# Three edits made together: the order of x's scalings and of h's sums at four seams, the stores of the derived output weights, and the last product of the output; with them, one tile in another bank and one order of products

## The chip, the cores and the metric

One core of a Trainium2 chip runs the whole program. The metric is the device time of one execution in microseconds (us), the median over several runs. TensorE is PE, VectorE DVE, ScalarE ACT, GpSimd POOL, SyncE SP (which here issues nearly all DMAs, in program order). All data are float32.

## The reference, cut to what matters

Attention with normalised q and k, then a feed-forward layer with a gate, over 8 sequences of 448 tokens, 12 heads of 64, model width 768, inner width 1536:

```python
q_n, k_n = rmsnorm(q, g_q), rmsnorm(k, g_k)          # q, k, v: (8, 12, 448, 64)
attn = softmax(q_n @ k_n.T / 8); o = attn @ v
x = o.transpose(0, 2, 1, 3).reshape(8 * 448, 768)
xn = x / sqrt(mean(x * x) + 1e-6) * rms_g
g = xn @ w_gate
out = (g * sigmoid(g) * (xn @ w_val)) @ w_out         # weights 768x1536, 1536x768
```

## The kernel before, in words

Attention is worked on by pairs of heads, six pairs a sequence. While PE does the attention of one sequence, it is also fed, between those steps, the feed-forward work of the sequences before. A list `todo` holds that work; `fill` (L1867) takes pieces from it, in proportion to their cost. All of the order is decided in Python when the program is built: `pe(fn)` (L382) counts a step, and `after(n, fn)` (L379) puts off a function by n steps. The engines then run their instructions in the order in which they were written, so the place in the order decides which operation waits behind which.

Let b be a sequence, 0 to 7. Its feed-forward work has two stages. *Gate and value* (`three`, L1413, matmul at L1408; for b = 0 `plain`, L1816) multiplies x by both weights in four groups of 15 products with sums of blocks (a 3x3 scheme of the Strassen kind); the results are h. Those sums of x, the tiles xs and top_x, are made on DVE at L989. *Output* multiplies h by w_out: plainly for b = 0 (`project_out`, L1544, matmul L1551); with the seven products of Strassen for b = 1 and b = 4 (`out_strassen`, L1630, matmul L1681); and for b = 2, 3, 5, 6, 7 in two levels (`out_quads`, L1696, matmul L1752), with seven outer products of seven inner ones. An outer product i goes in steps: a (two inner products, read at L1771 and L1772), b (L1778, L1779), c (L1789), and d (the last inner one, added into c's bank, read at L1801), with d of i behind a of i + 1. `finish` then combines whole outer products: mostly on POOL (L1723), the last of them on DVE (L1743), and `store` (L1578) writes out tiles. Sums of h are made at L1598 (first level, also called first_sums) and L1626 (second level).

A *seam* is where the attention of one sequence ends. There `rms_x` and `norm_x` (L943) norm x of the sequence just finished, `begin` (L1936) appends to the list the output of the sequence before it and then its own gate and value. So the seam of b = 1 falls on the output of b = 0, and the seam of b = 4 on the output of b = 3. Times in the profile: output of b = 0 at 239 to 285 us, gate and value of b = 1 285 to 408, its output 408 to 476; then 476 to 600 and 600 to 664 (b = 2), 664 to 785 and 785 to 846 (b = 3), 846 to 958 and 958 to 999 (b = 4), 1000 to 1112 and 1113 to 1176 (b = 5), 1177 to 1288 and 1289 to 1338 (b = 6), 1338 to 1427 and 1427 to 1476 (b = 7).

`norm_x` needs the factor of each token along the free dimension. For b up to 3 PE transposes it into a PSUM tile rb (L953), for later ones it is laid out in SBUF (tile ss). Six operations on DVE (`scale`, L959) then multiply x by it. For most seams `after` spreads them over the next two to four steps; for b = 7 they go to the list `slow`, ahead of the sums of x (L989), and `fill` takes one entry of `slow` per step when `first_sums` is empty. `first_sums` are handed out one per step, and two at b = 7's seam.

PSUM has eight banks: four in the pool ps_s (scores; tag "s"), one in ps_m, three in ps_f (everything of the feed-forward work; tag "f"). A tile takes the buffer of its pool that was given out longest ago and waits for that one's last reader. rb lies in ps_f for b = 0 and 1, in ps_s later.

The weights come in another format and are converted on the way (L1114 to L1185, POOL and DVE) while the first sequences run; converted blocks are kept in DRAM (`kept`, `kept_o`) and loaded again for each sequence (L1287, in `ask`, as soon as there is room). The sums of w_out's blocks for the two-level scheme are made on the chip by `derive_q` (L1356): 21 jobs of four DVE operations (L1371 to L1374), each with two blocks loaded (at L1267) and two blocks of its own, followed one step later by four stores to `kept_q`: two source blocks (L1378 and the first L1381) and two of sums. Jobs are spaced by three steps and run in `fill` alone. Blocks lie in one arena: kind "wg" takes four units of it from the low end, kind "w" three from the high end.

Of the kernel before, what the change touches and what calls it, by code (L numbers as in the profile page):

```python
# [8 lines left out]
F32 = mybir.dt.float32  # L9
# [326 lines left out]
def safe_scores(  # L336
# [606 lines left out]
    def norm_x(b):  # L943


        rs = st.pop(("rx", b))
        if late(b * NPAIR + NPAIR):
            ps = st.pop(("ss", b))
            nc.vector.transpose(out=blocks(ps), in_=rs.unsqueeze(2).to_broadcast([128, NB, 32]))
        else:  # L950
            ps = (ps_s if b > 1 else ps_f).tile([128, 512], F32, name="rb", tag="s" if b > 1 else "f")
            for t in range(NT):
                nc.tensor.transpose(ps[:, t * P:(t + 1) * P], rs[:, t:t + 1].to_broadcast([P, 128]), ident[0:P, 0:P])  # L953

        whole = st["x", b]

        def scale(hp):
            x = whole[:, hp, :]
            nc.vector.scalar_tensor_tensor(x, x, rg[:, hp:hp + 1], ps[:, 0:S], ALU.mult, ALU.mult)  # L959
# [24 lines left out]

        def op(name):
            first, second, what = LEFT_G[name]
            one, two = a[first], a[second]
            a[name] = place(name)
            nc.vector.tensor_tensor(a[name], one, two, what)  # L989
# [364 lines left out]
    todo_q = list(jobs_q)  # L1354

    def derive_q(wait=5):  # L1356

        if not todo_q or sums_o or now["t"] - asked.get("at_q", 0) < 3 or asked["n"] in next_gate or not room(2, "wg"):
            return False
# [15 lines left out]

        def store():
            parts = kept_q[i].rearrange("p (n w) -> p n w", w=HW)
            nc.sync.dma_start(out=parts[:, j], in_=x[:, 0])  # L1378
            for src, first, second in ((y, 1, 6), (ta, 2, 3), (tb, 4, 5)):
                gap = (second - first) * KG  # L1380
                nc.sync.dma_start(out=parts[:, first * KG + j:second * KG + j + 1:gap], in_=src)  # L1381
# [181 lines left out]

    def store(b, n, i, y):
        row0 = at = b * S + i * 128 - 64 * (b % 2)
        while at < row0 + 128:
# [9 lines left out]
            else:  # L1576
                rows = out[rows + col:rows + col + m, cols]
            nc.sync.dma_start(out=rows, in_=y[at - row0:at - row0 + m, :])  # L1578
            at += m
# [50 lines left out]
    def out_strassen(b):  # L1630
# [58 lines left out]
        pairs = out_pairs(b)  # L1689
        for name in ORDER_O:  # L1690
            for which in range(len(pairs)):
# [4 lines left out]
    def out_quads(b):  # L1696

        bank, dst, steps = {}, {}, []
        tiles = [i for pair in out_pairs(b) for i in pair]
        left = {}  # L1700
# [20 lines left out]
        def add(to, one, other):  # L1721
            for row in range(2):
                nc.gpsimd.tensor_tensor(to[row], one[row], other[row], ALU.add)  # L1723

        def finish(i):
            name, m = ORDER_Q[i], dst[i]
            if name == "B21":
                add(m, m, dst[0])
# [45 lines left out]
        def bb(i):  # L1774
# [4 lines left out]
            nc.vector.tensor_tensor(u[:, 1], ps[:, 1], u[:, 0], ALU.add)  # L1779
            st["no_x"] = now["t"]  # L1780
            left_q1(b, i, (3,))
            if i == 0 or i > 1 and i + 1 < len(ORDER_Q):
                left_q1(b, i + 1, (0,))

        def c(i):
            ps = two(i, "c")
            st["heavy"] = now["t"]
            u3 = st["u", b, i][:, 1:2].to_broadcast([128, 2, HW])
            nc.vector.tensor_tensor(dst[i][1].rearrange("p (h n) -> p h n", h=2), ps, u3, ALU.add)  # L1789
# [62 lines left out]
    def out_items(b):  # L1852
        if in_quads(b):
            return [(cost, TURNS, 0, fn) for cost, fn in out_quads(b)]
        if b >= FIRST_O:
            return [(NFP // 2 * HALF, TURNS, (0, ("wo", b, name, 3 * half + 2) if i == 0 else None), fn)
                    for (name, i, half), fn in zip(((name, i, half) for name in ORDER_O for i in range(len(out_pairs(b)))
                                                    for half in range(2)), out_strassen(b))]
# [8 lines left out]
    def fill(n=None, hold=False):  # L1867
# [8 lines left out]
        for left_over in reversed(range(min(n, len(todo)))):  # L1876
# [162 lines left out]
    for g in range(NG + 1):  # L2039
# [62 lines left out]
        else:  # L2102
# [92 lines left out]
```

## Time and profile before

| | us |
|---|---|
| median of 3 runs (lowest, highest) | 1487.42 (1486.82, 1487.74) |
| the profiled execution | 1486.21 |
| its span | 1484.4 |
| PE busy | 1456.5 (98%) |
| DVE, ACT, POOL busy | 1071.3, 619.5, 764.4 |
| moved by DMA | 322.5 MB, of it 320.6 MB on SP's queue |

The span is the time from the first to the last instruction of the profiled execution; 1.81 us of its time lie outside. A row of the timeline gives the start, the duration, engine, line, operation, output and inputs (partitions x elements), how many it merges, and in brackets how long the engine had been idle before it and who released it. PE's ends are modelled, so that its busy time is an upper figure.

### The profile page before, as it was taken

Reading aid. Unit: us, or ns where it says so; the run is one execution under the profiler, and the core shown is the slowest. Engines: PE = TensorE matmul, PEld = TensorE weight load, DVE = VectorE, ACT = ScalarE, POOL = GpSimd, SP = SyncE. Lnnn points to the kernel's source line nnn. Section 1 sums busy time; section 2 is a strip of 40 time slices with the busy share of each in tenths; the row PEclk is TensorE's granted clock in tenths of the full one; section 3 lists DMA queues with packets and bytes.
Section 4 is the critical chain, followed back from the end, with each engine's and each line's share of the span. In section 5 each row is a group of like instructions: output and inputs, shape, how many; then the busy total and the mean of one; then the engine's idle time right before and its main releaser. Section 6 shows DMA issues by size and latency. Waiting matters only on the chain.

```text
span 1484.4 us, 25739 instructions
## 1 busy us (share of the span) xinstructions
PE 1456.5 (98%) x8538; PEld 1141.9 (77%) x8538; DVE 1071.3 (72%) x1866; ACT 619.5 (42%) x1551; POOL 764.4 (51%) x684
## 2 busy tenths in 40 slices
PE   8999999999999999999999999999999999999997
PEld 4344444678855788888888889859898799899997
DVE  6788999699874677874579855755679756774664
ACT  7856776445523444234433443444542533101200
POOL 6877987647353363463545744645645842130002
PEclk9999999999999999999999999999999999999999
DMA  8758686676877899987566966677467855597675
GB/s 215 226 156 252 180 242 179 209 245 219 264 226 223 263 310 314 297 283 208 141 170 194 280 178 184 183 212 210 128 188 230 270 171 149 163 307 234 172 226 193
DMA packets 340577, 322.52 MB, mean 217 GB/s; under 512 B 126932, under 2 KB 282068, under 8 KB 340436
## 3 DMA queue, kind: packets, MB, share of 16 engines
q1 hardware_dynamic: 339508, 320.58, 72.4%
q8 instruction: 71, 1.16, 0.3%
q14 instruction: 70, 0.57, 0.1%
q10 hardware_dynamic: 800, 0.20, 0.1%
q0 software_dynamic: 128, 0.00, 0.0%
HBM read 266.90 MB, written 53.77 MB: 216 GB/s over the span
## 4 chain that ended last, share of the span: by engine, by line
PE 82%; DVE 11%; DMA 3%; issue 2%; SPq 1%; ACT 0%; POOL 0%; DVEq 0%; ACTq 0%; POOLq 0%
PE ff L1408 36%; PE ff L1752 13%; PE sc L805 8%; PE ff L1826 6%; PE av L823 6%; PE ff L1681 6%; PE ff L1551 2%; DMA w<-kept 2%; PE sc L705 1%; PE av L732 1%; PE den L749 1%; PE tr L684 1%; PE den L887 1%; DVE l L1626 1%; DVE x L959 1%
## 5 line engine op out<-in xcount | busy, mean ns | idle before, releaser
L909 POOL TENSOR_TENSOR es<-es,e 128x448 f32<-128x448 f32 x205 | 255.1, 1245 | 13.6
L1408 PE MATMUL ff<-x,w 128*128 128x224 f32 x1296 | 258.1, 353 | 0.3 <-DVE pc L1429 0.3
L1408 PEld LDWEIGHTS ff<-x,w 128*128 128x128 f32 x1296 | 243.6, 190 | 3.5 <-issue 2.1
L805 PE MATMUL sc<-qT,kT 64*64 64x448 f32 x1176 | 231.1, 539 | 0.0
L823 PE MATMUL av<-e,yard 64*64 64x448 f32 x1148 | 223.8, 538 | 0.0
L1408 PE MATMUL ff<-xs,w 128*128 128x224 f32 x832 | 164.7, 353 | 3.8 <-DMA w<-kept 3.1
L1408 PEld LDWEIGHTS ff<-xs,w 128*128 128x128 f32 x832 | 156.1, 190 | 7.7 <-issue 3.9
L805 PEld LDWEIGHTS sc<-qT,kT 64*64 64x64 f32 x1176 | 78.8, 133 | 86.1 <-issue 54.8
L786 POOL TENSOR_TENSOR ss<-ss,rd 128x448 f32<-128x448 f32 x40 | 47.6, 1191 | 159.4 <-ACT rd L785 158.0
L1752 PE MATMUL ff<-w,l 128*128 128x192 f32 x630 | 117.2, 329 | 4.5 <-DVE l L1626 2.2
L1429 DVE TENSOR_TENSOR pc<-ff,l 128x448 f32<-128x448 f32 x56 | 34.9, 622 | 108.6 <-PE ff L1408 77.8
L1826 PE MATMUL ff<-x,w 128*128 128x448 f32 x288 | 111.8, 541 | 0.0
L1752 PEld LDWEIGHTS ff<-w,l 128*128 128x128 f32 x630 | 103.8, 190 | 10.0 <-DVE l L1626 3.0
L823 PEld LDWEIGHTS av<-e,yard 64*64 64x64 f32 x1148 | 77.3, 133 | 36.9 <-issue 36.7
L904 POOL TENSOR_TENSOR es<-e 128x448 f32<-128x448 f32 x41 | 48.5, 1182 | 110.2 <-ACT e L813 79.9
L813 ACT ACTIVATE e<-sc 128x448 f32<-128x448 f32 x168 | 88.0, 547 | 36.5 <-PE sc L805 27.1
L1826 PEld LDWEIGHTS ff<-x,w 128*128 128x128 f32 x288 | 53.3, 190 | 51.1 <-issue 48.0
L811 ACT ACTIVATE e<-sc,yard 128x448 f32<-128x448 f32 x126 | 78.2, 634 | 32.7 <-PE sc L805 24.2
L1408 PE MATMUL ff<-top_x,w 128*128 128x224 f32 x440 | 91.1, 356 | 0.0
L1408 PEld LDWEIGHTS ff<-top_x,w 128*128 128x128 f32 x440 | 81.8, 190 | 11.5 <-issue 10.6
L1426 DVE TENSOR_TENSOR pb<-ff,pb 128x448 f32<-128x448 f32 x84 | 52.3, 622 | 47.8 <-PE ff L1408 47.7
L1723 POOL TENSOR_TENSOR y<-y,pa 128x384 f32<-128x384 f32 x10 | 11.1, 1127 | 144.6 <-DVE y L1801 137.2
(244 smaller groups left out, 2972.4 us busy)
## 6 DMA issues: line engine op xcount, KB each, us to landing
w<-kept SPq DMA_DIRECT2D x380, 256.0 KB, 3.9
w<-kept_q SPq DMA_DIRECT2D x350, 192.0 KB, 3.8
w<-kept_o SPq DMA_DIRECT2D x150, 192.0 KB, 3.8
kept_q<-w SPq DMA_DIRECT2D x63, 192.0 KB, 3.6
raw<-in_moe_w_gate_dram SPq DMA_DIRECT2D x24, 384.0 KB, 4.7
raw<-in_moe_w_val_dram SPq DMA_DIRECT2D x24, 384.0 KB, 4.2
kept<-w SPq DMA_DIRECT2D x48, 192.0 KB, 4.3
raw<-in_moe_w_out_dram SPq DMA_DIRECT2D x24, 384.0 KB, 3.7
```

Source lines behind the costliest of these rows:

```text
L786: after(m, lambda: (nc.gpsimd.tensor_tensor(ss, ss, rd, ALU.add), st.update({("summed", b): hp})))
L805: nc.tensor.matmul(ps[r, 0:S], lhsT=keys(g, r, i), rhs=st["qT", g][r, :], start=True, stop=True)
L811: nc.scalar.activation(e, ps[:, 0:S], ACT.Exp, scale=st["rs", g][:, NB + i:NB + i + 1])
L813: nc.scalar.activation(e, ps[:, 0:S], ACT.Exp)
L823: nc.tensor.matmul(st["av", g][own(j), 0:S], lhsT=vt, rhs=st["e", g, i][r], start=i == 0, stop=i == PARTS - 1, skip_group_check=True)
L904: nc.gpsimd.tensor_tensor(st["es", g], st["e", g, 0], st["e", g, 1], ALU.add)
L909: nc.gpsimd.tensor_tensor(st["es", g], st["es", g], st["e", g, i], ALU.add)
L1408: nc.tensor.matmul(bank[:, w * HT:(w + 1) * HT], lhsT=data(key)[:, (2 * w + c) * 128:(2 * w + c + 1) * 128], rhs=a[left][:, c, :], start=o ...
L1426: nc.vector.tensor_tensor(T[name], ps[:, 0:S], T[name], ALU.add)
L1681: nc.tensor.matmul(ps, lhsT=left_o(b, which, LEFT_O[name], c), rhs=data(("wo", b, name, c)), start=first and c == 0, stop=c == NFP - 1, sk ...
L1752: nc.tensor.matmul(ps, lhsT=a[:, j, :], rhs=data(key)[:, n % 2 * HW:(n % 2 + 1) * HW], start=start and j == 0, stop=j == KG - 1, skip_grou ...
L1826: nc.tensor.matmul(bank[w][:, 0:S], lhsT=data(key)[:, c * 128:(c + 1) * 128], rhs=st["x", 0][:, 3 * half + c, :], start=half == c == 0, st ...
```

## The change

Five places are touched.

1. `norm_x` of b = 1 puts rb into ps_s.
2. For b = 3 to 6 the six scalings of x go into the list `slow`, as they did for b = 7, and `first_sums` are handed out two per step in every two-level output.
3. The output of b = 4, which has one pair of row tiles, runs its seven products in ORDER (B11, T2, B21, T3, T1, T4, B22) and loads its weights so; before, in ORDER_O (B11, B21, T2, T3, T1, B22, T4). B21 adds onto the bank of B11. In ORDER, B22 still adds onto the bank of T1.
4. `derive_q` stores the two source blocks at once and the two blocks of sums three steps later (all four were one step later); takes "w" blocks for the sums until the next gate's loads begin; is spaced by four steps until then; may run while those loads are asked for, if three "wg" blocks are free; gives up its own blocks after six steps; and is also called between attention steps.
5. In the output of b = 7, the last outer product (i = 6) is combined otherwise: POOL adds the product before it into rows of the third and fourth (`split_sum`), DVE adds that to parts of the last product as they are made, d gets a fresh bank, and the last tile is stored by two queues, SP and ACT, 64 rows each.

The diff, cut to its core:

```diff
@@ norm_x
-            ps = (ps_s if b > 1 else ps_f).tile([128, 512], F32, name="rb", tag="s" if b > 1 else "f")
+            ps = (ps_s if b else ps_f).tile([128, 512], F32, name="rb", tag="s" if b else "f")
...
-            if b == B - 1:
+            if b > 2:
                 slow.append(("x", lambda hp=hp: scale(hp)))
             elif b:
-                after(hp // 3 if b == 1 else hp // 2 + (2 if b > 2 else 0), lambda hp=hp: scale(hp))
+                after(hp // (3 if b == 1 else 2), lambda hp=hp: scale(hp))
...
-        st["x_at"] = now["t"] - (NPAIR if b == B - 1 else 0)
+        st["x_at"] = now["t"] - (NPAIR if b > 2 else 0)
@@ the order of the weights' loads, of out_strassen's steps and of out_items
+    def order_o(b):
+        return ORDER_O if len(out_pairs(b)) > 1 else ORDER
...
-            for name in ORDER_O:
+            for name in order_o(b):
@@ derive_q
+    def own_kind():
+        return "w" if asked["n"] <= next_gate[0] else "wg"
...
-        if not todo_q or sums_o or now["t"] - asked.get("at_q", 0) < 3 or asked["n"] in next_gate or not room(2, "wg"):
+        if not todo_q or sums_o or now["t"] - asked.get("at_q", 0) < (4 if asked["n"] <= next_gate[0] else 3) or asked["n"] in next_gate and not room(3, "wg") or not room(2, own_kind()):
             return False
...
-        st[own_a], st[own_b] = block("wg"), block("wg")
+        st[own_a], st[own_b] = block(own_kind()), block(own_kind())
...
-        after(1, store)
+        nc.sync.dma_start(out=parts[:, j], in_=x[:, 0])
+        store(y, 1, 6)
+        after(3, store_sums)
         for key in (*keys, own_a, own_b):
-            after(7 if i and key[0] != "wx" else 4, lambda key=key: used(key))
+            after(6 if key[0] != "wx" else 4, lambda key=key: used(key))
@@ store
-            nc.sync.dma_start(out=rows, in_=y[at - row0:at - row0 + m, :])
+            queues.pop(0).dma_start(out=rows, in_=y[at - row0:at - row0 + m, :])
@@ out_quads
+        end = len(ORDER_Q) - 1 if b == B - 1 else None
...
+        def split_sum(row):
+            m = dst[end - 1][row]
+            nc.gpsimd.tensor_tensor(dst[2][row], dst[2][row], m, ALU.add)
+            nc.gpsimd.tensor_tensor(dst[3][row], dst[3][row], m, ALU.add)
+            after(1, lambda: store(b, 1, tiles[2 + row], dst[3][row]))
...
+            if end and i == end - 1:
+                split_sum(0)
+                left_q1(b, end, (3,))
+                half = lo_hi(dst[end][0])[0]
+                nc.vector.tensor_tensor(half, half, lo_hi(dst[2][0])[0], ALU.add)
+            elif end and i == end:
+                store(b, 1, tiles[0], m[0], (nc.sync, nc.scalar))
@@ out_quads, bb
+            if end and i == end:
+                nc.vector.tensor_tensor(u[:, 0], u[:, 0], lo_hi(dst[2][0])[1], ALU.add)
+                both = dst[2][1].rearrange("p (h n) -> p h n", h=2)
+                nc.vector.tensor_tensor(both, both, u[:, 1:2].to_broadcast([128, 2, HW]), ALU.add)
+                return
@@ out_quads, c
+            if end and i == end:
+                half = st["u", b, i][:, 0]
+                nc.vector.tensor_tensor(half, ps[:, 1], half, ALU.add)
+                nc.vector.tensor_tensor(dst[i][1].rearrange("p (h n) -> p h n", h=2), ps,
+                                        dst[2][1].rearrange("p (h n) -> p h n", h=2), ALU.add)
+                store(b, 1, tiles[1], dst[i][1])
+                return
...
+            if end and i == end - 1:
+                split_sum(1)
@@ out_quads, d
-            ps = bank[i, "c"]
-            term(i, 6, ps[:, 1], start=False)
+            if end and i == end:
+                ps = ps_f.tile([128, 512], F32, name="ff", tag="f")[:, 0:BW].rearrange("p (h n) -> p h n", h=2)
+            else:
+                ps = bank[i, "c"]
+            term(i, 6, ps[:, 1], start=bool(end) and i == end)
@@ fill
-                for _ in range(min(len(first_sums), 2 if st["quads"] == B - 2 else 1)):
+                for _ in range(min(len(first_sums), 2 if st["quads"] > 1 else 1)):
@@ the loop over pairs of heads, between attention steps
             pe(lambda: [step(g, i) for i in (1, 2)])
+            derive_q()
             pe(lambda: [step(g, i) for i in (3, 4)])
```

Line numbers in the orders below are each kernel's own; in the changed kernel L1610, L1638, L1798, L1804, L1827 and L1844 are the L1598, L1626, L1772, L1778, L1789 and L1801 of before.

DVE at the start of the two-level output of b = 3 (785 us), before. L959 are scalings of x, L1598 and L1626 sums of h, h_116 to h_118 the tiles of h, raw and l the sums:

```order
958 L959 SCALAR_TENSOR_TENSOR x<-x,rg,ss 128x448 x2
959 L1598 TENSOR_TENSOR raw<-h_116,h_118 128x384
960 L1789 TENSOR_TENSOR pa<-ff,th 128x384
961 L1626 TENSOR_TENSOR l_7124<-l_7108,h_117 128x384
962 L1626 TENSOR_TENSOR h_117<-h_117 128x3x128
963 L959 SCALAR_TENSOR_TENSOR x<-x,rg,ss 128x448 x2
964 L1598 TENSOR_TENSOR raw<-raw,h_116 128x384
965 L1772 TENSOR_TENSOR y<-ff,th 128x192
966 L959 SCALAR_TENSOR_TENSOR x<-x,rg,ss 128x448 x2
```

The same place in the changed kernel:

```order
959 L1638 TENSOR_TENSOR l_7107<-h_116,l_6987 128x384
960 L1638 TENSOR_TENSOR l_7109<-h_117,h_118 128x384
961 L1610 TENSOR_TENSOR raw<-h_116,h_118 128x384
962 L1610 TENSOR_TENSOR raw<-raw,h_116 128x384
963 L1827 TENSOR_TENSOR pa<-ff,th 128x384
964 L1638 TENSOR_TENSOR l_7124<-l_7109,h_117 128x384
965 L1638 TENSOR_TENSOR h_117<-h_117 128x3x128
966 L1610 TENSOR_TENSOR h_116<-h_116 128x3x128
967 L1610 TENSOR_TENSOR raw<-h_118,raw 128x384
```

The pairs of scalings between the sums of h are gone from there; the first-level sums (L1610) come two at a time, and one scaling stands ahead of the piece shown.

DVE at the end of the same stage (about 840 us), before: what stands ahead of and behind the last second-level sum l_7653, which the d step of the last outer product reads (y and pa are products, yard and kT belong to the attention):

```order
1034 L1626 TENSOR_TENSOR raw<-raw 128x384
1035 L1772 TENSOR_TENSOR y<-ff,th 128x192
1036 L506 STREAM_TRANSPOSE yard<-yard 128x448
1037 L1801 TENSOR_TENSOR pa<-ff,th 128x192
1038 L471 TENSOR_REDUCE yard<-sq 128x14
1039 L1778 TENSOR_TENSOR th<-ff,th 128x192
1040 L1779 TENSOR_TENSOR th<-ff,th 128x192
1041 L1626 TENSOR_TENSOR l_7653<-raw,l_7601 128x384
1042 L1789 TENSOR_TENSOR y<-ff,th 128x384
1043 L471 TENSOR_REDUCE yard<-sq 128x14
```

The same place in the changed kernel, where that sum is l_7652:

```order
1035 L1638 TENSOR_TENSOR raw<-raw 128x384
1036 L989 TENSOR_TENSOR xs<-x 128x448
1037 L1798 TENSOR_TENSOR y<-ff,th 128x192
1038 L506 STREAM_TRANSPOSE yard<-yard 128x448
1039 L989 TENSOR_TENSOR xs<-x 128x448
1040 L1844 TENSOR_TENSOR pa<-ff,th 128x192
1041 L471 TENSOR_REDUCE yard<-sq 128x14
1042 L989 TENSOR_TENSOR top_x<-x,xs 128x448
1043 L1804 TENSOR_TENSOR th<-ff,th 128x192
1044 L1805 TENSOR_TENSOR th<-ff,th 128x192
1045 L1638 TENSOR_TENSOR l_7652<-raw,l_7595 128x384
1046 L1827 TENSOR_TENSOR y<-ff,th 128x384
```

Sums of x (xs, top_x) that had been made earlier in the stage now stand around it: three ahead of l_7652 and one behind.

SP in the output of b = 1, at the first job of `derive_q` (w<-kept_o are loads of weights, kept_q<-w stores of a job), before:

```order
304 L1287 DMA w<-kept_o 128x384 x6
305 L1578 DMA out_dram<-y 64x384 x2
306 L1378 DMA kept_q<-w 128x192
307 L1381 DMA kept_q<-w 128x2x192 x3
308 L1287 DMA w<-kept_o 128x384 x3
309 L1267 DMA w<-kept_o 128x384 x2
310 L1287 DMA w<-kept_o 128x384 x3
```

And in the changed kernel, where the first job comes earlier:

```order
298 L1290 DMA w<-kept_o 128x384 x2
299 L1393 DMA kept_q<-w 128x192
300 L1386 DMA kept_q<-w 128x2x192
301 L1290 DMA w<-kept_o 128x384
302 L527 DMA yard<-in_q_dram 128x2x192
303 L531 DMA yard<-in_k_dram 128x3x64 x2
304 L1290 DMA w<-kept_o 128x384 x3
305 L1386 DMA kept_q<-w 128x2x192 x2
```

The four stores that stood in one piece are two and two, with loads between.

More of the change, by code (lines that the diff above doesn't have):

```diff
@@ L1374, in derive_q, with store, store_sums @@
         nc.vector.tensor_tensor(tb[:, 0], y[:, 0], ta[:, 0], ALU.subtract)
[L1376 to L1381, printed above, removed]
+        parts = kept_q[i].rearrange("p (n w) -> p n w", w=HW)
+        def store(src, first, second):
+            gap = (second - first) * KG
+            nc.sync.dma_start(out=parts[:, first * KG + j:second * KG + j + 1:gap], in_=src)
+        def store_sums():
+            store(ta, 2, 3)
+            store(tb, 4, 5)
             asked["sums_q"] = asked.get("sums_q", 0) + 1
-        after(1, store)
+        nc.sync.dma_start(out=parts[:, j], in_=x[:, 0])
+        store(y, 1, 6)
+        after(3, store_sums)
         for key in (*keys, own_a, own_b):
-            after(7 if i and key[0] != "wx" else 4, lambda key=key: used(key))
+            after(6 if key[0] != "wx" else 4, lambda key=key: used(key))
         return True
@@ L1562, in project_out, with store @@
         store(b, n, i, y)
-    def store(b, n, i, y):
+    def store(b, n, i, y, queues=(nc.sync, nc.sync)):
+        queues = list(queues)
         row0 = at = b * S + i * 128 - 64 * (b % 2)
@@ L1689, in out_strassen @@
         pairs = out_pairs(b)
-        for name in ORDER_O:
+        for name in order_o(b):
             for which in range(len(pairs)):
@@ L1723, in add @@
                 nc.gpsimd.tensor_tensor(to[row], one[row], other[row], ALU.add)
+        def split_sum(row):
[3 more added lines that the diff above has]
+            after(1, lambda: store(b, 1, tiles[2 + row], dst[3][row]))
         def finish(i):
             name, m = ORDER_Q[i], dst[i]
-            if name == "B21":
+            if end and i == end - 1:
[5 more added lines that the diff above has]
+                store(b, 1, tiles[0], m[0], (nc.sync, nc.scalar))
+            elif name == "B21":
                 add(m, m, dst[0])
@@ L1856, in out_items @@
             return [(NFP // 2 * HALF, TURNS, (0, ("wo", b, name, 3 * half + 2) if i == 0 else None), fn)
-                    for (name, i, half), fn in zip(((name, i, half) for name in ORDER_O for i in range(len(out_pairs(b)))
+                    for (name, i, half), fn in zip(((name, i, half) for name in order_o(b) for i in range(len(out_pairs(b)))
                                                     for half in range(2)), out_strassen(b))]
```

## The prediction

> **What bounds the kernel now.** I read the page first: its busy times, then the chain that ended last.
>
> ```profile
> span 1484.4 us, 25739 instructions
> PE 1456.5 (98%) x8538; PEld 1141.9 (77%) x8538; DVE 1071.3 (72%) x1866; ACT 619.5 (42%) x1551; POOL 764.4 (51%) x684
> PE 82%; DVE 11%; DMA 3%; issue 2%; SPq 1%; ACT 0%; POOL 0%; DVEq 0%; ACTq 0%; POOLq 0%
> ```
>
> PE is the bound at 98%, and the change leaves its matmuls as they are (only one of the output stages issues the same ones in another order). So what can be won is 1484.4 − 1456.5 = 27.9 us in which PE is idle, plus time in which it is busy at a lower clock; both ends of the program are in that. The table by stretches says where it lies.
>
> ```profile
> core 0: us, PE busy (x) PEld busy (x) DVE busy (x) ACT busy (x) POOL busy (x), PEclk, DMA share, GB/s
> 240.00:245.00 5.00, 5.00 (x12) 2.67 (x11) 4.93 (x7) 1.00 (x2) 4.92 (x7) 0.66 0.39 96
> 340.00:360.00 20.00, 18.95 (x115) 16.49 (x117) 19.68 (x28) 10.99 (x45) 15.35 (x13) 1.00 0.48 161
> 476.00:600.00 124.00, 119.77 (x754) 101.35 (x753) 91.03 (x181) 51.79 (x117) 54.32 (x51) 1.00 0.93 296
> 600.00:664.00 64.00, 62.36 (x430) 53.37 (x429) 52.98 (x102) 19.42 (x49) 34.07 (x32) 1.00 0.93 296
> 785.00:846.00 61.00, 59.52 (x405) 50.39 (x404) 56.13 (x99) 19.64 (x43) 41.11 (x32) 1.00 0.80 229
> 836.00:846.00 10.00, 9.85 (x58) 9.26 (x57) 9.42 (x14) 1.66 (x3) 9.62 (x9) 1.00 0.84 238
> 1113.00:1177.00 64.00, 62.90 (x427) 54.05 (x426) 58.41 (x104) 20.82 (x47) 43.87 (x36) 1.00 0.82 245
> 1167.00:1177.00 10.00, 9.85 (x58) 9.26 (x57) 8.70 (x14) 2.41 (x6) 9.62 (x10) 1.00 0.94 286
> 1289.00:1338.00 49.00, 49.00 (x301) 48.84 (x300) 39.45 (x85) 3.25 (x9) 14.20 (x17) 1.00 0.91 297
> ```
>
> PE idles 4.23 us in 476–600, 1.64 in 600–664, 1.48 and 1.10 in the two later quarter-block stages. DVE is all but full in places (19.68 of 20 us; 9.42 of 10): there a wait that is removed can come back as DVE time.
>
> **The tile rb (first seam).** Timeline around the wait, and the row 240–245 above:
>
> ```profile
> 238.63 0.61 DVE L1835 SCALAR_TENSOR_TENSOR h<-th,ff 128x448 f32<-128x448 f32 x1
> 239.30 6.15 PE L1551 MATMUL ff<-w,h 128*128 128x384 f32 x13 [2.36 <-DVE h L1835]
> 245.04 2.44 DVE L959 SCALAR_TENSOR_TENSOR x<-x,rg,rb 128x448 f32<-128x448 f32 x4
> 248.93 0.59 PE L805 MATMUL sc<-qT,kT 64*64 64x448 f32 x2
> ```
>
> The three banks of ps_f hold the last gate, the last value and rb, so the first output tile must wait for L1835, which reads that gate. With rb in ps_s the tile takes a bank free since before: 2.36 us go. The granted clock of 0.66 over the next 5 us cost 5 × 0.34 = 1.7 us; it followed this wait at once, so I let it go too: 4.1 us. Against it: rb now holds one of four score banks until the last x scaling ends (245.04 + 2.44 = 247.5). Scores that began at 248.93 would begin near 248.93 − 4.1 = 244.8, use three banks in some 2 us, and wait about 0.7 us for the fourth. Bounds: −4.1, and +0.7 if DVE, which does conversions here, gives nothing earlier. I take −3.2, near the end that the removed wait itself shows.
>
> [...] If the drop were not this wait's doing, the clock's 1.7 us would stay and the sum would be 1.7 us smaller.
>
> **derive_q.** The waits of PE in its stretch, and SP's:
>
> ```profile
> 510.36 1.75 PE L1408 MATMUL ff<-xs,w 128*128 128x224 f32 x8 [1.80 <-DMA w<-kept]
> 573.59 1.75 PE L1408 MATMUL ff<-xs,w 128*128 128x224 f32 x8 [0.79 <-DMA w<-kept]
> 599.17 1.78 PE L1408 MATMUL ff<-raw,w 128*128 128x224 f32 x8 [0.81 <-DVE pb L1426]
> 607.52 0.76 PE L1752 MATMUL ff<-w,l 128*128 128x192 f32 x3 [0.96 <-DMA w<-kept_q]
> SPq L1381 <- DVE w L1374: 19.4, 12, 5.1
> L1371 DVE TENSOR_TENSOR w<-w x21: 341/350/1284, 432.9 to 602.0; 128x192 f32<-128x192 f32 x21
> ```
>
> SP issues in order. It stands 19.4 us (twelve times) at the stores of a job's sums, waiting for DVE, with weight loads behind it. Now the sources go out at once and the sums three steps later, when DVE is done: the weight loads pass. Jobs also begin about three earlier, so the last three of 21 (up to 602.0) leave the place where they sat ahead of L1426 and of the first quarter-block loads. The four rows add to 4.4 us; all idleness of both stretches is 5.9. But the DMA share there is 0.93: what is late because DMA engines are full stays late. Each job still costs DVE 4 × 0.35 = 1.4 us, now partly inside the attention steps, where DVE has room (91 of 124 us). What can get worse: jobs in the output stage ahead take "w" blocks, which its loads of kept_o want too, and its stores go past those loads on SP. Bounds −5.9 and +1 (one load held up as long as the 0.96 us wait above). I take −3.0, some two thirds of the four rows: the waits behind SP's standing and behind DVE's jobs.
>
> **x behind the sums of h.** These rows are a stage's begin (two), a contended L1626, and what the moved operations cost:
>
> ```profile
> 805.41 1.24 PE L1752 MATMUL ff<-w,l 128*128 128x192 f32 x6 [1.22 <-DVE l L1626]
> 1135.59 1.24 PE L1752 MATMUL ff<-w,l 128*128 128x192 f32 x6 [0.95 <-DVE l L1626]
> L959 DVE SCALAR_TENSOR_TENSOR x<-x,rg,ss x24: 669/680/1557, 789.4 to 1311.4; 128x448 f32<-128x448 f32 x24
> L989 DVE TENSOR_TENSOR xs<-x x28: 574/615/1555, 264.6 to 1319.0; 128x448 f32<-128x448 f32 x28
> L909 POOL TENSOR_TENSOR es<-es,e 128x448 f32<-128x448 f32 x205 | 255.1, 1245 | 13.6
> 839.46 1.48 DVE L1626 TENSOR_TENSOR raw<-raw 128x384 f32<-128x384 f32 x1
> 843.11 1.36 DVE L1626 TENSOR_TENSOR l<-raw,l 128x384 f32<-128x384 f32 x1
> 845.54 1.14 PE L1752 MATMUL ff<-w,l 128*128 128x192 f32 x6
> ```
>
> Six scalings of 0.68 us leave the road to the first L1626 sums, so 1.22 + 0.95 = 2.2 us go. They are not saved, only later: everything in the slow list moves back by six places, and three sums (two xs, one top_x) now stand ahead of the last product's L1626, where none stood. POOL is busy 9.62 of 10 us there and two-input adds take 1.4 instead of 0.55. Three sums cost 3 × 0.61 = 1.8 to 3 × 1.555 = 4.7 us; the old L1626 ended at 843.11 + 1.36 = 844.47, and its matmul began at 845.54, so 1.07 us is cover. Loss per stage: 0.8 to 3.6 us. I take 2.0 for 785–846, less (1.2) for 1113–1177, where DVE is at 8.70, and 0.5 for 600–664, whose start has a DMA wait anyway. Sum −2.2 + 3.7 = +1.5; bounds −2.2 and +3 × 3.6 − 2.2 = +8.6. The last seam (1289–1338) already works like this and PE never idles there, but POOL is busy 14.20 of 49 us: it doesn't decide.
>
> [...]
>
> **Order of the fifth sequence's output (958–1000).**
>
> ```profile
> 963.32 0.91 PE L1681 MATMUL ff<-w,h 128*128 128x384 f32 x2 [0.57 <-ACT pa L1660]
> 985.34 2.85 PE L1681 MATMUL ff<-w,raw 128*128 128x384 f32 x8 [0.65 <-DVE y L1653]
> ```
>
> With one pair of tiles, B21 stood right behind B11 in the same bank and had to wait for the copy of B11, and T4 behind B22 likewise. The new order puts another product (six matmuls) between: 1.2 us go, nothing new is late. Bounds −1.2 and 0.
>
> **The end.**
>
> ```profile
> 1471.22 1.95 POOL L1723 TENSOR_TENSOR pc<-pc,pa 128x384 f32<-128x384 f32 x2 [4.88 <-DVE pa L1801]
> 1472.67 0.36 DVE L1778 TENSOR_TENSOR th<-ff,th 128x192 f32<-128x192 f32 x1 [1.59 <-PE ff L1752]
> 1473.34 1.21 DVE L1626 TENSOR_TENSOR l<-raw,l 128x384 f32<-128x384 f32 x1
> 1475.29 1.24 PE L1752 MATMUL ff<-w,l 128*128 128x192 f32 x6 [0.71 <-DVE y L1789]
> 1477.03 1.03 DVE L1743 TENSOR_TENSOR y<-y,pa 128x384 f32<-128x384 f32 x2
> 1477.62 1.80 SPq L1578 DMA_DIRECT2D out_dram<-y  x3
> ```
>
> The d product gets a bank of its own and doesn't wait for the adds of the c product: 0.71. New is a DVE add that waits for POOL's add of the row's tiles: that ends about 1471.22 + 0.98 = 1472.2, and what is queued behind it on DVE, L1778, has to wait for PE until 1472.67 anyway; without that half microsecond of cover it would cost what it is late. The two adds after the last matmul (1.03) are done earlier on POOL and DVE. Three issues in a row took 1.80 us; the whole tile now goes ahead, and the last tile's halves by two queues at once, so one issue of 0.6 follows the last add: about 0.9 less, since adds and issues overlapped by a little. Together −2.6; bounds −1.7 (the second queue no faster) and −3.5.
>
> **The sum.** −3.2 − 3.0 + 1.5 − 1.2 − 2.6 = −8.5. The profiled execution took 1486.21 us with its 1484.4 of span: 1477.7. The median of the runs is 1487.42, so 1.2 more: 1478.9, and I say 1479.
>
> **Rivals.** *Given back.* Behind the first seam DVE is at 19.68 of 20, and DMA at 0.93 of 476–664. Then rb brings 1 instead of 3.2, derive_q 1 instead of 3.0: 1483. For it: those two rows. Against: SP's 19.4 us are no lack of bandwidth. *It does not do what it says*: x behind the sums only moves the waits, at the +8.6 end, with the rest as forecast: 1487.4 + 8.6 − 10.0 = 1486, no change. *Slower.* The same place, but PE's new waits of up to 3.6 us exceed the 2.36 us that came ahead of the clock's drop, so each of three stages pays another 1.7: 8.6 + 5.1 = 13.7 against −10.0, 1491. It decides from about 2.4 us of wait in each of the three. Against it: the median sum takes 0.615, and DVE, freed of x at the stages' starts, comes earlier to their ends. [...] *All goes well*: SP's waits and the clock were everything and x costs nothing: −4.1 − 5.9 − 2.2 − 1.2 − 3.5 = −16.9, 1470.5.
>
> **Chances.** Forecast (1475 to 1482) 0.57; given back 0.22; all well 0.06; not as it says 0.09; slower 0.06. 0.2% is 3 us, about what a measurement here tells from no change. So faster by over that: 0.85, within 0.09, slower 0.06. The range 1472.5 to 1485 leaves out the slow cases and the best end.
>
> **What would show it.** Right: no wait of PE at L1551 after the first seam and a granted clock of 1.00 there; SPq L1381 waits under 5 us; no L1626 wait at a quarter-block stage's start, but waits of 0.5 to 2 us for l or y in its last two products; none at L1681 in 958–1000; L1743's last two adds gone and the end about 2.6 us closer to the last attention. Wrong: PE waits for w<-kept as long as before (then DMA engines were the cause), or waits over 2.4 us with a clock below 1.00 at the stages' ends.

## The result and the profile after

The changed kernel takes 1476.95 us (median of 6 runs, 1476.14 to 1477.38), the kernel before 1486.76 beside it (6 runs). The ratio is 0.9936, with a 95% interval of 0.9923 to 0.9948: 9.8 us faster, where 8.5 were forecast. The time that was forecast, 1479 us, is 2 us too long; 0.7 of that lies in the kernel before, whose median over six runs is 1486.76 and not the 1487.42 of the first three. The profiled execution took 1476.63 us.

The page of the changed kernel, its span and busy times:

```profile
span 1474.8 us, 25744 instructions
PE 1453.6 (99%) x8538; PEld 1141.6 (77%) x8538; DVE 1074.3 (73%) x1868; ACT 619.6 (42%) x1551; POOL 764.8 (52%) x684
```

PE issues the same 8538 matmuls. So the traces can be laid side by side: the start of the n-th matmul of one against that of the n-th of the other (the order differs only in the output of b = 4). How far ahead the changed kernel is, and where it gains (+) or loses (−):

| place in the kernel before, us | change | ahead |
|---|---|---|
| start to 236 | +0.25 | 0.25 |
| first output tile, 236 to 244 | +4.3 | 4.55 |
| fourth score tile, 251 | −0.7 | 3.8 |
| 510; 574; 599; 608 | +1.1; +1.0; +1.1; +1.2 | 8.3 |
| start of the output of b = 3, 803 to 806 | +1.9 | 10.2 |
| its end, 842 to 846 | −2.0 | 8.3 |
| output of b = 4, 963 and 985 | +0.8; +0.9 | 10.1 |
| first group of gate and value of b = 5, 1010 to 1013 | −1.9 | 8.2 |
| start of the output of b = 5, 1136 | +1.2 | 9.4 |
| its end, 1172 to 1176 | −2.0 | 7.5 |
| last inner product, 1475 | +1.0 | 8.5 |
| behind the last matmul | +1.1 | 9.6 |

Steps of 0.1 us that stand between these places are only in the column on the right. The first row is scatter: a second profile of the changed kernel has 0.0 there.

Against the rows shown of before: the table by stretches of the changed kernel (PE, PEld, DVE, ACT, POOL busy, granted clock, DMA share, GB/s).

```profile
236.00:240.00 4.00, 4.00 (x16) 2.49 (x15) 3.86 (x8) 1.05 (x3) 3.83 (x3) 1.00 0.82 229
240.00:245.00 5.00, 5.00 (x22) 2.64 (x24) 4.93 (x8) 1.49 (x3) 4.92 (x7) 1.00 0.40 96
476.00:600.00 124.00, 122.34 (x781) 105.49 (x774) 91.27 (x183) 51.84 (x118) 55.02 (x53) 1.00 0.97 312
828.00:838.00 10.00, 8.41 (x46) 7.17 (x45) 9.97 (x16) 1.94 (x3) 7.69 (x7) 1.00 0.80 237
952.00:994.00 42.00, 42.00 (x224) 23.74 (x223) 21.32 (x38) 17.38 (x36) 23.75 (x21) 1.00 0.79 236
995.00:1008.00 13.00, 11.64 (x61) 10.97 (x60) 9.38 (x17) 4.16 (x13) 8.77 (x7) 1.00 0.87 253
1420.00:1468.00 48.00, 48.00 (x296) 47.72 (x294) 35.20 (x78) 2.76 (x8) 12.51 (x12) 1.00 0.76 250
```

PE is full and at full clock behind the first seam. In 476–600 it idles 1.66 us (124 − 122.34) instead of 4.23, although the DMA engines are busier than before (0.97). The output of b = 4 and the end have no idle time left. What is new are two holes: PE works 8.41 of 10 us at the end of the output of b = 3, with DVE at 9.97, and 11.64 of 13 at the beginning of b = 5's gate and value. Before, PE had no idle time at the second of these places:

```profile
1005.00:1018.00 13.00, 13.00 (x73) 12.72 (x75) 9.07 (x17) 4.22 (x13) 8.70 (x7) 1.00 0.86 249
```

The timeline of the changed kernel at the first of these holes, POOL, DVE and PE:

```profile
826.02 5.67 POOL L909 TENSOR_TENSOR es<-es,e 128x448 f32<-128x448 f32 x4
830.62 1.55 DVE L989 TENSOR_TENSOR xs<-x 128x448 f32<-128x448 f32 x1
832.09 0.34 DVE L1798 TENSOR_TENSOR y<-ff,th 128x192 f32<-128x192 f32 x1
832.49 1.24 PE L1778 MATMUL ff<-w,raw 128*128 128x192 f32 x6 [0.49 <-DVE y L1798]
832.92 0.57 DVE L989 TENSOR_TENSOR xs<-x 128x448 f32<-128x448 f32 x1
834.21 1.10 DVE L989 TENSOR_TENSOR top_x<-x,xs 128x448 f32<-128x448 f32 x1
836.51 0.54 DVE L1827 TENSOR_TENSOR y<-ff,th 128x384 f32<-128x384 f32 x1
837.11 1.08 PE L1778 MATMUL ff<-w,l 128*128 128x192 f32 x5 [0.89 <-DVE y L1827]
```

The sums of x (L989) stand ahead of the reads that free PSUM banks (L1798, L1827), and PE waits for these reads. The first of them takes 1.55 us beside POOL, which is busy to 826.02 + 5.67 = 831.69; the next, at 832.92 with POOL idle, takes 0.57.

The second hole, PE and DVE:

```profile
1000.55 0.61 DVE L989 TENSOR_TENSOR l<-x,top_x 128x448 f32<-128x448 f32 x1
1001.27 3.27 PE L1419 MATMUL ff<-l,w 128*128 128x224 f32 x16 [1.04 <-ACT yard L486]
1004.85 3.48 PE L1419 MATMUL ff<-x,w 128*128 128x224 f32 x17 [0.32 <-DVE x L989]
```

The bracket names ACT, but the matmul's input is the tile l, and the sum that writes it ends at 1000.55 + 0.61 = 1001.16, just ahead of it. Where a releaser makes no sense, look at who wrote the operand.

### The profile page after: what moved, and what is told of

It is laid out like the page before. It is cut to its first block, busy times and chain, and to the rows that moved or that the text cites. A ratio compares the mean times of both kernels' runs of the same rounds, so it can differ in the third digit from the quotient of the medians.

```text
span 1474.8 us, 25744 instructions
## 1 busy us (share of the span) xinstructions
PE 1453.6 (99%) x8538; PEld 1141.6 (77%) x8538; DVE 1074.3 (73%) x1868; ACT 619.6 (42%) x1551; POOL 764.8 (52%) x684
## 2 busy tenths in 40 slices
DMA packets 340577, 322.52 MB, mean 219 GB/s; under 512 B 126932, under 2 KB 282068, under 8 KB 340436
## 4 chain that ended last, share of the span: by engine, by line
## 5 line engine op out<-in xcount | busy, mean ns | idle before, releaser
L1778 PE MATMUL ff<-w,l 128*128 128x192 f32 x630 | 116.2, 328 | 2.4 <-DVE y L1827 1.8
L1778 PEld LDWEIGHTS ff<-w,l 128*128 128x128 f32 x630 | 103.8, 190 | 7.0 <-DVE y L1827 2.5
L1419 PE MATMUL ff<-l,w 128*128 128x224 f32 x416 | 83.7, 354 | 1.2 <-ACT yard L486 1.0
```

What stands on the lines that cost most here:

```text
L1419: nc.tensor.matmul(bank[:, w * HT:(w + 1) * HT], lhsT=data(key)[:, (2 * w + c) * 128:(2 * w + c + 1) * 128], rhs=a[left][:, c, :], start=o ...
L1778: nc.tensor.matmul(ps, lhsT=a[:, j, :], rhs=data(key)[:, n % 2 * HW:(n % 2 + 1) * HW], start=start and j == 0, stop=j == KG - 1, skip_grou ...
```

## Experiments

Theory: the table's rows are separate effects of separate edits, that add. Rival: the edits need each other (a gain given back on a full DVE or full DMA engines; a loss that only looks like x's). A number like "1.7 us of the trace" below is from the same matching of matmuls.

**The edits alone, on the kernel before.** e1_rb:

```diff
-            ps = (ps_s if b > 1 else ps_f).tile([128, 512], F32, name="rb", tag="s" if b > 1 else "f")
+            ps = (ps_s if b else ps_f).tile([128, 512], F32, name="rb", tag="s" if b else "f")
```

> The kernel before with rb in ps_s at the first seam and nothing else. If the parts simply add, as matching the two traces matmul by matmul says: no wait of PE at L1551, the granted clock 1.00 in 240 to 245 us, 4.1 us won up to the first output tile, 0.5 given back at the fourth score tile, 3.6 us in all: 1483.1 us. If what is won there is given back further on, where DVE is full: 1485 to 1486.5. If the drop of the clock was not that wait's doing, the clock still drops somewhere near there and 1.7 us less are won.

Measured: 1482.67 against 1485.80 us, ratio 0.9978 (0.9968 to 0.9987), 3.1 us faster. In the trace 4.3 are won at the first output tile and 0.7 given back at the fourth score tile, 3.6 in all, as expected; later stretches differ by up to 0.8 us up and down.

e2_derive puts in the new `derive_q` and its call between attention steps, and nothing else:

> The kernel before with the new derive_q and its call between attention steps, nothing else. If the parts add: the four waits at 508, 572, 598 and 606 us go, 4.4 us, 1482.3 us. If these went only because the first seam had moved everything ahead of them: 0 to 2 us, 1485 to 1487. The wait of PE at L1551 is still there; if it always draws the clock down behind it, the clock in the 5 us after it is again about 0.66; if the drop hangs on when the wait falls, it may be 1.00 here.

Measured: 1482.70 us, ratio 0.9980 (0.9971 to 0.9990), 3.1 us faster. The four waits go, 0.9, 1.0, 1.1 and 1.2 us of the trace, less 0.3 lost at 614 us, with the wait at the first seam as it was. So they don't hang on the other edits. But 1.7 us of this trace were won where nothing had been changed: at the first seam PE waited 2.38 us as before, and the clock stayed at 1.00. More on this below.

e3_x puts in the edits to `scale`, `x_at` and the number of h's sums per step, and nothing else:

> The kernel before with x scaled behind the sums of h at the seams of b = 3 to 6 and two sums of h per step, nothing else. If the parts add: 1.2 to 1.9 us won at the starts of the outputs of b = 3 and b = 5, 1.8 lost at each of their ends and 1.8 at the start of the gate and value of b = 5: 2.3 us slower, 1489.1 us. If the losses belong to the other parts (they move where transfers and the attention's sums fall): 2 to 3 us faster, 1484.

Measured: 1488.38 us, ratio 1.0014 (1.0004 to 1.0024), 2.6 us slower. In its trace: 1.9 and 1.2 won at the starts, 2.0 and 2.0 lost at the ends, 1.9 lost at 1010 us. This part of the change is a loss, and one of its own.

e4_end_order puts in `order_o` and the new end, and nothing else:

> The kernel before with the new combination of the last outer product and with ORDER in the output of b = 4, nothing else. If the parts add: 1.65 us won in 958 to 1000, 0.9 at the last inner product, 1.1 behind the last matmul: 3.7 us, 1483.1 us. If the end is set by the writes' landing and not by how many issues go ahead: only 2.6 us, 1484.2.

Measured: 1481.43 us, ratio 0.9965 (0.9951 to 0.9979), 4.4 us faster. Its trace shows 1.8 us in the output of b = 4, 1.0 at the last inner product, 1.1 behind the last matmul, and a span that is 4.0 us shorter.

The four medians add to −3.1 − 3.1 + 2.6 − 4.4 = −8.0, the whole change gave −9.8 and, in another set of runs below, −8.6. Within what these medians can tell, the edits add.

**x's part taken out of the changed kernel.** Beside one another: the changed kernel again, and three with x's part undone in whole or in part.

> The changed kernel once more, as the reference for the three beside it: 1477 us, and 8.9 to 9.8 us under the kernel before. Both theories say the same.

Measured: 1477.71 us, the kernel before 1486.35, ratio 0.9940 (0.9927 to 0.9953).

e5_no_x:

```diff
-            if b > 2:
+            if b == B - 1:
... (the steps of the scalings and `x_at` likewise as before)
-                for _ in range(min(len(first_sums), 2 if st["quads"] > 1 else 1)):
+                for _ in range(min(len(first_sums), 2 if st["quads"] == B - 2 else 1)):
```

> The changed kernel with x scaled as before at the seams of b = 3 to 6 and one sum of h per step, all else as changed. If that part is a loss that stands by itself (its own run was 2.6 us slower than the kernel before): 2.4 us faster than the changed kernel, 1474.5 us, with the waits at L1638 back at the starts of the outputs of b = 3 and 5 and none at their ends. If the other parts need it, because they made the rest earlier and DVE later against it: as the changed kernel or slower, 1477 to 1479.

Measured: 1475.12 us, ratio to before 0.9924 (0.9910 to 0.9938): 2.6 us less than the changed kernel, as its own run had said. The waits at the starts are back (1.9 and 1.2 us of the trace), those at the ends and at 1000 us are gone (2.0, 2.0 and 1.9).

e6_sums_only undoes x's order and keeps two sums of h per step:

> The changed kernel with x scaled as before, but two sums of h per step as changed. If the gain at the starts came from the sums that are given out faster: the starts' waits stay away, the ends' losses go, 1473 us. If it came from x being out of the way: waits of 1 us or more at the starts as before, none at the ends, 1474.5.

Measured: 1479.98 us, ratio 0.9957 (0.9944 to 0.9971): neither. It is 4.9 us slower than with both undone. The waits of PE in its output of b = 2:

```profile
PE sc L805 <- DVE x L959: 2.1, 1, 2.1
PE ff L1778 <- DVE pa L1827: 0.5, 1, 0.5
PE ff L1778 <- DVE raw L1638: 0.2, 1, 0.2
```

With sums of h ahead of them, the scalings come late, and here they read rb, which holds one of the four score banks: the attention's scores wait 2.1 us. At the other two starts its trace loses 2.5 and 1.8 us against the changed kernel, where undoing both lost 1.9 and 1.2. So twice the sums is a loss without x behind them. The other half, x behind the sums with one sum per step, was not run; that it needs the second sum is not shown.

e7_no5 undoes the order at b = 5's seam alone:

```diff
-            if b > 2:
+            if b > 2 and b != 5:
...
-                after(hp // (3 if b == 1 else 2), lambda hp=hp: scale(hp))
+                after(hp // (3 if b == 1 else 2) + (2 if b == 5 else 0), lambda hp=hp: scale(hp))
... (`x_at` likewise)
```

> The changed kernel with x scaled as before at the seam of b = 5 alone, which falls on the output of b = 4 (no two-level products, no sums of h to go ahead). If the 1.8 us lost at the start of the gate and value of b = 5 are that seam's scalings: 1475.2 us and no wait of PE at about 1000 us. If they come from the new order of products in the output of b = 4: no change, 1477.

Measured: 1475.55 us, ratio 0.9927 (0.9914 to 0.9941), 2.2 us less than the changed kernel, 1.9 of the trace. Its row for the second hole:

```profile
995.00:1008.00 13.00, 13.00 (x73) 12.30 (x76) 9.36 (x17) 3.64 (x12) 8.12 (x7) 1.00 0.83 235
```

The hole is that seam's. There are no sums of h to hand out there; moving the scalings back only makes the sums of x late for the products that read them.

**What made the weights late.** e8_stores, on the kernel before, only splits a job's stores:

```diff
-            nc.sync.dma_start(out=parts[:, j], in_=x[:, 0])
-            for src, first, second in ((y, 1, 6), (ta, 2, 3), (tb, 4, 5)):
+            for src, first, second in ((ta, 2, 3), (tb, 4, 5)):
...
+        nc.sync.dma_start(out=parts[:, j], in_=x[:, 0])
+        nc.sync.dma_start(out=parts[:, KG + j:6 * KG + j + 1:5 * KG], in_=y)
...
-        after(1, store)
+        after(3, store)
```

> The kernel before with derive_q's stores alone split: the two source blocks at once, the two of sums after three steps; jobs start when they did, keep their kind of block and end where they did. If SP's standing was the cause of the waits for w<-kept: those at 508 and 572 us go (1.9 us), those at 598 and 606 (the last three jobs) stay, 1483.9 us. If the DMA engines were the cause, being busy 0.93 of the time: all stay, 1485.8. If only the earlier start matters, the same.

Measured: 1482.83 against 1486.08 us, ratio 0.9977 (0.9968 to 0.9987): 3.3 us, as much as all of `derive_q`'s edits (by the traces 3.1 against 3.7). The rows of PE's waits for weights and for the job's DVE work in 476 to 610 us in this kernel (total, times, longest):

```profile
PE ff L1410 <- DMA w<-kept: 0.9, 2, 0.7
PE ff L1410 <- DVE pb L1428: 0.8, 1, 0.8
PE ff L1754 <- DMA w<-kept_q: 0.3, 1, 0.3
```

And SP's longest, in 476 to 606:

```profile
SPq L1383 <- DVE w L1374: 14.0, 8, 4.3
```

The waits at 508, 572 and also 606 go or shrink (1.1, 1.0 and 1.2 us of the trace, less 0.7 lost at 609), the one for DVE at 598 stays. I had expected the one at 606 to stay with the last three jobs: it went with the stores as well. That SP still stands 14.0 us in all, for all of the gain, shows that the sum of a queue's standing says little. What counts, I take it, is which loads are behind it when it stands. In the changed kernel the rows of the same view read:

```profile
SPq L1386 <- DVE w L1380: 4.4, 4, 2.3
SPq L1290 <- PE ff L1419: 3.4, 7, 0.6
SPq L1270 <- DMA kept_q<-w: 3.1, 6, 1.1
```

**The end.** e9_one_queue:

```diff
-                store(b, 1, tiles[0], m[0], (nc.sync, nc.scalar))
+                store(b, 1, tiles[0], m[0])
```

> The changed kernel with both halves of the last tile stored by SP, one behind the other. If the number of issues behind the last add sets the end: 0.45 us more, 1477.9 us. If the landing of the writes sets it (the halves issued together took 2.7 us, where the stores before took 2.2 to 2.4): no difference, 1477.4.

Measured: 1478.20 us, ratio to before 0.9947 (0.9933 to 0.9960), where the changed kernel had 0.9940 and 0.9936: the runs alone can't tell it. From the end of the last add (1469.13 of 1476.3 us) its span goes on for 7.2 us, in the changed kernel for 6.3 (1468.55 of 1474.8). In the seven other traces with both queues that is 5.8 to 6.3 us, so the second queue is worth some 0.9 to 1.3 us, with one profile for the one queue. Both accounts fell short: the last issue ends 0.64 us later there, and the halves also take longer to land, 3.8 us where the changed kernel's (shown below) took 2.7:

```profile
out_dram<-y SPq DMA_DIRECT2D x2, 96.0 KB, 3.8
```

**Can both be had?** e10_hold keeps the gain at the starts and moves three sums of x out of the way of the ends; b = 5's seam is as in e7_no5:

```diff
+            if b < B - 2:
+                st["hold_x"] = i == len(ORDER_Q) - 2
...
-            elif slow and now["t"] != st.get("no_x") and ...
+            elif slow and not st.get("hold_x") and now["t"] != st.get("no_x") and ...
```

> The changed kernel with the seam of b = 5 as before, and in the two-level outputs of b = 2, 3 and 5 no sum of x is made between the sixth product's c step and the last one's b step; those three sums follow behind the last c step. If the losses at the ends of these stages come from sums of x that stand ahead of the last evacuations on a full DVE: the starts' gains stay and the ends' losses of 1.8 us each go, 3.6 us under the kernel without the seam of b = 5 (1475.5), so 1472 us. If DVE has simply as much work as the stage is long, the same waits come back some us later, at the first products of the next gate and value, for L989: 1475.5 or more.

Measured: 1476.93 us, ratio 0.9941 (0.9927 to 0.9955): no better than the changed kernel and 1.4 us worse than e7_no5. The ends' losses are gone (no wait of PE in 785 to 850), but PE now waits three times for sums of x (total, times, longest):

```profile
PE ff L1419 <- DVE x L989: 3.3, 3, 1.2
```

The one behind the output of b = 3, DVE and PE (the others are at 678 and 1186 us):

```profile
851.34 0.62 DVE L1440 TENSOR_TENSOR pc<-ff,l 128x448 f32<-128x448 f32 x1 [7.54 <-DMA yard<-in_q_dram]
856.36 0.61 DVE L989 TENSOR_TENSOR x<-x 128x448 f32<-128x448 f32 x1
857.03 4.24 PE L1419 MATMUL ff<-x,w 128*128 128x224 f32 x21 [1.25 <-DVE x L989]
```

PE waits for a sum of x that is made at the last moment, and DVE had just stood idle for 7.54 us, in the attention's steps, where nothing is handed out. So it is not the amount of DVE's work. e11_caught_up hands out three more there:

```diff
             derive_q()
+            for _ in range(st.pop("late_x", 0)):
+                if slow and may_make(slow[0][0]):
+                    slow.pop(0)[1]()
             pe(lambda: [step(g, i) for i in (3, 4)])
```

> The kernel of the run before (seam of b = 5 as in the kernel before; three sums of x kept out of the last two products' evacuations), and three more sums of x made in the attention steps behind the two-level output, where DVE had stood idle for 7.5 us while PE later waited 1.25 us for a sum of x. If the losses were a matter of the order on DVE and not of the amount of its work: the waits at 857 and 1187 us go too, 3.5 us under the kernel without the seam of b = 5 (1475.55), so 1472.1 us, under both kernels. If DVE's work is the bound there: other waits of the same size, 1475 or more.

Measured: 1471.12 against 1486.59 us, ratio 0.9898 (0.9881 to 0.9914): 15.5 us under the kernel before, and about 6 under the change. The row of its output of b = 3:

```profile
780.00:841.00 61.00, 60.80 (x413) 52.34 (x412) 56.70 (x99) 21.80 (x51) 41.76 (x34) 1.00 0.80 235
```

DVE is as busy there as before (56.70 of 61 us, against 56.13), and PE idles 0.2 us instead of 1.48.

## Why the prediction was right, point by point

| step | forecast | trace | its own run |
|---|---|---|---|
| rb | −3.2 | −3.6 | −3.1 |
| `derive_q` | −3.0 | −4.5 | −3.1 |
| x behind the sums of h | +1.5 | +2.6 | +2.6 |
| order, output of b = 4 | −1.2 | −1.8 | −4.4 with the end |
| the end | −2.6 | −2.0 | |

*rb.* Wait and clock went, and the price at the fourth score tile was 0.7, as forecast (0.5 of it a wait of PE). The clock's 1.7 us come with this wait, but not in each execution (in two of five traces): see the last section. The median of the kernel before holds them only in part, which fits that e1_rb's own run gave 3.1 and its trace 3.6.

*derive_q.* The mechanism was right: SP's standing, not the bandwidth, since the same bytes (322.52 MB in all) moved at a DMA share of 0.97 without the waits. The wait at 599 alone is not SP's: e8_stores keeps it, e2_derive with its earlier jobs does not. By this trace the size was too small: I let a third of the four rows stay as DMA's, and all went. By the medians, 3.1 and 3.3 us (e2_derive, e8_stores), it was right, and it need not be all each time: in a second profile of the changed kernel a wait of 0.82 us for w<-kept is back at 504 us.

*x.* Sign and place were right for the quarter-block (two-level) outputs: the start's waits go, worth 1.9 and 1.2 us of the trace where the brackets gave 1.22 and 0.95, and waits of 0.5 and 0.9 us for L1798 and L1827 come in the last two products. The three sums of x ahead took 1.55, 0.57 and 1.10 us, 3.2 in all, within the bounds of 1.8 and 4.7. (The longest add of two inputs on DVE in the trace of before takes 1.60 us, a little over the 1.555 of the prediction's row for L989.) The forecast losses were 2.0, 1.2 and 0.5; they were 2.0, 2.0 and none. What failed is the step "three stages": the seam of b = 5, where the scalings were moved too, is not in the sum. The output it falls on has no sums of h, and it cost 1.9 us alone, more than the whole miss of this term (1.1).

*Order.* Both waits went. The matching, which goes by the starts of the matmuls, gives 1.8 us where the brackets (idle times counted from PE's modelled ends) gave 1.2, as it does for the waits of x; what fills the difference is not settled.

*The end.* The wait behind c's adds went (1.0 by the matching, 0.71 in the bracket), and the new wait of DVE for POOL (0.89 us of idle time) was hidden, as forecast: PE has 48.00 of 48 us. Behind the last matmul 1.1 came instead of 1.9. The timeline and the DMA view of the changed kernel at the end:

```profile
1468.20 0.35 DVE L1844 TENSOR_TENSOR y<-ff,th 128x192 f32<-128x192 f32 x1
1468.58 0.57 ACTq L1590 DMA_DIRECT2D out_dram<-y  x1
```

```profile
out_dram<-y ACTq DMA_DIRECT2D x1, 96.0 KB, 2.7
out_dram<-y SPq DMA_DIRECT2D x1, 96.0 KB, 2.7
```

The halves, issued together, land after 2.7 us, where the last stores of before took 2.2 and 2.4. What was mis-sized is the shorter line of issues, forecast at 0.9. From the last matmul to the end of the last add the changed kernel takes 0.53 us where the kernel before took 1.53: the two adds, 1.0 as forecast. From the last add to the end of the span it takes 6.3 us against 6.4, so the issues brought 0.1 here; over all traces it is 5.8 to 6.3 us in eight with the new end against 6.3 to 7.1 in five with the old, 0.5 us less on average. The last issue ends 0.7 us sooner behind the last add, and part of that went into the longer landing.

*Rivals.* Nothing was given back behind the first seam: the matching stays at 3.8 us ahead from 251 to 508. x's losses stayed at 2.0 a stage, in waits of 0.9 us at most, and the clock stayed at 1.00 there. The errors of the terms by the trace, −0.4, −1.5, +1.1, −0.6 and +0.6, partly cancel; a total that is right to 1.3 us is some luck.

## What to carry to other kernels

Where an engine serves two readers in program order, moving work out of the way of one puts it in the way of the other (here 1.9 and 1.2 us won at the starts, 2.0 and 2.0 lost at the ends). Look for the stretch in which that engine stands idle, and hand the work out there: here the same work cost 2.6 us when it was moved as a block, and won about 4 (1471.1 against 1475.1 with it left in its place) when its last pieces were put into the attention's steps and the seam of b = 5 was left as it was. A store that waits for another engine doesn't belong ahead of loads in one queue: write it behind them, some steps later (3.3 us in e8_stores), and judge it by the loads that stand behind it and not by how long the queue stands. And if two kernels issue the same instructions on the engine that bounds them, match them one by one: that gives every gain and loss of that pair of traces its place, to about a tenth of a microsecond, where medians only tell the sum. What another execution does differently (0.82 us at 504 above, the clock below) only further traces tell.

## What the runs showed of the hardware

The same wait came with a drop of the clock in two profiled executions of five. All five have it, PE's wait at the first seam, 2.34 to 2.38 us long; it begins at 236.7 to 236.9 us and ends at 239.0 to 239.3. Kernel before, stretches of 2 us:

```profile
239.00:241.00 2.00, 1.70 (x5) 1.00 (x6) 1.93 (x6) 0.00 (x0) 1.92 (x3) 0.88 0.68 244
241.00:243.00 2.00, 2.00 (x5) 1.09 (x4) 1.93 (x4) 0.55 (x2) 2.00 (x3) 0.50 0.00 0
243.00:245.00 2.00, 2.00 (x6) 1.07 (x6) 2.00 (x3) 0.46 (x2) 2.00 (x3) 0.77 0.73 145
```

e4_end_order, where the clock drops earlier:

```profile
237.00:239.00 2.00, 0.00 (x0) 0.00 (x0) 1.93 (x6) 1.01 (x2) 1.92 (x2) 0.94 0.72 142
239.00:241.00 2.00, 1.91 (x3) 1.18 (x4) 1.93 (x6) 0.00 (x0) 1.92 (x3) 0.50 0.56 217
241.00:243.00 2.00, 2.00 (x6) 1.09 (x5) 1.93 (x3) 0.76 (x2) 2.00 (x3) 0.71 0.00 0
```

e2_derive, where it stays:

```profile
239.00:241.00 2.00, 1.77 (x6) 1.11 (x7) 1.93 (x6) 0.00 (x0) 1.92 (x3) 1.00 0.60 229
241.00:243.00 2.00, 2.00 (x8) 1.21 (x7) 1.93 (x3) 0.62 (x2) 2.00 (x3) 1.00 0.00 0
```

In the first the clock is at half from 240.5 to 243.9 us (0.88 over two microseconds is 0.48 us at half speed, 0.77 is 0.92), in the second from 238.8 to 242.2: 3.4 us both times, 1.7 us apart. In the third, and likewise in e3_x and e8_stores, it doesn't drop: 1.00 in each stretch from 237 to 245 us. So the wait is worth 2.4 us, and with the drop about 4.1.

What decides whether it drops is not shown. The wait ends at 239.30 and 239.09 us in the two traces with the drop (the kernel before, e4_end_order) and at 239.23, 239.14 and 239.03 us in the three without (e2_derive, e8_stores, e3_x): neither its length nor its place in the trace tells them apart. Nor does the drop begin at one distance from it: 1.2 us behind its end in the first, 0.3 us ahead of its end in the second. In six traces with rb in ps_s (the changed kernel twice, e1_rb, e5_no_x, e6_sums_only, e7_no5) the clock is 1.00 from 236 to 245 us.

Part of the scatter of the kernel before (1484.0 to 1488.3 us in one set of 26 runs, the changed kernel's twelve runs 1476.1 to 1479.0) may be this drop. Of its 58 executions in the four sets of runs beside the experiments, 34 have a mean granted clock of 0.997 or less and a median of 1486.4 us, the other 24 one of 1485.5. That is a hint only, since the mean also counts the half clock behind the last matmul: 0.78 in 1479 to 1480 us and 0.50 from there to the end in the kernel before, 0.97 in 1472 to 1473 us and 0.50 from there on in the changed kernel, which has no other drop.
